# Joining the squares of k's four token blocks before the head norm matmul, in a kernel of two attention and two Fourier layers

## The chip, the core and the metric

The kernel runs on one core of a Trainium2 chip. The metric is the device time of one execution in microseconds (us); for the kernel before it is 2460.21 us, the median of three runs (2456.98 to 2460.39).

## What is computed

x has 2048 tokens of 640 features. Twice in a row it goes through an attention block and a Fourier block, each with a layer norm in front and a residual added.

```python
def _A_ref(x, wqkv, wo):                      # H = 32 heads of Dh = 20
    qkv = (x @ wqkv).reshape(B, S, 3, H, Dh) ...
    q, k, v = qkv[0], qkv[1], qkv[2]
    scores = einsum("bhqd,bhkd->bhqk", q, k) * (Dh ** -0.5)
    p = softmax(scores, axis=-1)
    o = einsum("bhqk,bhkd->bhqd", p, v)
    return o...reshape(B, S, D) @ wo
x = x + _A_ref(_layernorm(x), A_wqkv, A_wo)
x = x + _B_ref(_layernorm(x), ...)            # Real(DFT_seq(DFT_hidden(x)))
x = x + _A_ref(_layernorm(x), A_wqkv, A_wo)
x = x + _B_ref(_layernorm(x), ...)
```

The kernel doesn't look for the largest score of a row before it takes exponentials. It uses a bound instead: a score is no larger than the length of the head's q times the length of its k, so the largest squared norm of q and of k over all tokens, head by head, gives a shift that is safe for every row. These norms are what the change is about.

## The kernel before, in words

**Tiling.** Tokens are worked on in four blocks of 512 (NB = 4, the index tb), features in five chunks of 128 (ND = 5). q and k are held with features on partitions: a product of 15 matmuls (five feature chunks, three passes each, line 195) gives 128 features of q or of k for 512 tokens in one psum bank, the tile `pqk`. There are five such chunks of q (c = 0 to 4) and five of k (c = 5 to 9). A head has 20 features, so a chunk of 128 holds parts of seven or eight heads.

**keep** (line 198) takes a finished `pqk` out of psum as a rounded part and a remainder (the tile `hl`), has POOL issue the DMA that stores it in memory (line 211), and makes the squares `sq` in bf16. In the prologue ACT makes the rounded part and the squares (line 208) and VectorE the remainder (line 209); in the last token block ACT does the squares first. In the attention VectorE does all three in the order rounded part (line 88), remainder (line 91), squares (line 205).

**norms** (line 214) multiplies the squares by `ind`, a 0/1 matrix from 128 features to 32 heads (line 216): the result `pn`, 32 heads by 512 tokens in psum, holds each token's share of each head's squared norm. VectorE takes the maximum over the 512 tokens (line 217) into one column of `top`, which has a column for each of q and k, chunk and token block. **bounds** (line 434) takes the maximum over the blocks, adds over the chunks, and multiplies q's with k's. **bound** (line 442) makes the shift from it and sends it to memory for four heads; the loads of q take it from there as two further rows. At the end a flag is set if, for all 32 heads, the product stays within (30 / SCALE)^2 with SCALE = 20 ** -0.5 (line 426); the program runs its general path over both layers again if a flag is missing.

**Prologue** (line 279). Chunk 0 of q and chunk 0 of k are done for all four token blocks. In each block TensorE does two products, then turns the next block's x (line 167), then the two norms (line 363), then four value products `pv` of 15 matmuls; in the first block the value products come ahead of the turning. The last block has nothing to turn, so its norms follow the products directly. Psum tiles of the prologue go round eight banks, one further with each tile (line 161). After the last block come the first bound and its shift.

**Attention.** The steps go through 8 groups of four heads, 4 blocks of 512 queries and 16 tiles of 128 keys: 512 steps per layer. A step has two score tiles `psc` of two matmuls each (line 522), two exponentials on ACT (line 525) and four value matmuls into the accumulator `acc` (line 533), which stand side by side in four groups of 32 output columns. At the end of a query block VectorE transposes the accumulator (line 540) and scales it. psum holds three double banks for scores, one bank for `acc` and one, `fill`, for everything else.

The rest of q, k and v is made between these steps, on TensorE's instruction stream, in an order written out beforehand (lines 387 to 425): chunks 1 of k, 1 of q, 2 of k, 2 of q, then the second half of v, then 3 of k, 3 of q, 4 of k, 4 of q, each for four token blocks. Up to step 236 strings like "ssfsssvvsssvvsssfssvvsssnvv" say where scores (s), value matmuls (v), halves of a product (f) and the norm (n) stand; later a product comes in three pieces. The norm of a block is placed two steps behind its product up to step 236 and four steps behind it afterwards (line 641). VectorE also compares pieces of the transform matrices along the whole attention (lines 803 and 807). `fill` here is also the name of a pool of SBUF tiles, with one buffer for each tag, `hl` and `sq` among them.

Of the kernel before, what the change touches and what calls it, by code (L numbers as in the profile page):

```python
# [7 lines left out]
BF = mybir.dt.bfloat16  # L8
I32 = mybir.dt.int32
AF = mybir.ActivationFunctionType  # L10
OP = mybir.AluOpType
# [4 lines left out]
S, D, H, DH = 2048, 640, 32, 20  # L16
# [3 lines left out]
ND = D // 128  # L20
NT = S // 128
NB = S // 512
# [17 lines left out]
def mha_fnet_kernel(ctx, tc, x_in, wqk, wv, wo, seq, hid, nat_seq, nat_hid, out):  # L40
# [33 lines left out]
    def bank(tag, shape, name):  # L74
        return pools["pool"].tile(list(shape), F32, name=name, tag=tag)
# [60 lines left out]
    class Qkv:  # L136
        def __init__(s, L, src):
            s.L, s.src = L, src
            s.xn, s.xt, s.rs, s.v = {}, {}, {}, {}
            s.scr = {qk: dr.tile([D, 2, S], F32, name=f"scr{qk}_{L}") for qk in "qk"}  # L140
            s.shift = {n: dr.tile([H, 2, c], F32, name=f"shift{n}_{L}") for n, c in (("b", 512), ("m", S))}
            s.n = 1
            s.made, s.raw, s.silent = set(), {}, False
# [54 lines left out]
        def keep(s, p, c, tb, vector, room):  # L198

            hl = room("hl", [2, 512], F32R, "hl")  # L200
            sq = room("sq", [512], BF, "sq")
            h = hl[:, 0].bitcast(F32)
            if vector:
                split(hl[:, 0], hl[:, 1], p, vector)
                V.tensor_tensor(sq, h, h, op=OP.mult)
            else:
                for f, x in ((AF.Copy, hl[:, 0]), (AF.Square, sq))[::-1 if tb == NB - 1 else 1]:
                    A.activation(x, p, f)
                V.tensor_tensor(hl[:, 1], p, h, op=OP.subtract)
            k, c = divmod(c, ND)  # L210
            G.dma_start(s.scr["qk"[k]][c * 128:(c + 1) * 128, :, tb * 512:(tb + 1) * 512], hl.bitcast(F32))  # L211
            return sq

        def norms(s, p, c, tb, sq):

            PE.matmul(p, ind[:, c % ND], sq, start=True, stop=True)  # L216
            V.tensor_reduce(s.top[:H, c // ND, c % ND, tb:tb + 1], p, op=OP.max, axis=AX.X)  # L217

# [60 lines left out]
        def prologue(s, vals, xt, fill, att):  # L279
# [50 lines left out]
            for tb in range(NB):  # L330

                sq, late = [], tb == 0
                if late:
                    for k in range(2):
                        later(tb, k, s.load)
                for k in range(2):
                    p = s.bank([128, 512], "pqk")
                    for dc in range(ND):
                        for f in s.product(p, s.w[k], tb, dc):
                            f()  # L340
                    sq.append(s.keep(p, k * ND, tb, False, (room, fill)[k]))
                    if late:
                        s.stats(2 + k)
                        continue
                    later(tb, k, s.stats)
                if late:
                    for n in range(4):
                        own(tb, n)
                        if n < 2:
                            s.norm(2 + n)  # L350
                            later(tb, n, s.stats)
                if tb == 0:
                    att.setup()
                elif tb == 1:
                    for t in range(NT - ND, NT):
                        ones(t)
                if tb + 1 < NB:
                    s.turn(tb + 1)
                    for k in range(2):
                        later(tb + 1, k, s.load)  # L360
                for k in range(2):
                    later(tb, k, s.norm)
                    s.norms(s.bank([H, 512], "pn"), k * ND, tb, sq[k])
                if tb == 0:
                    att.qload(0, 0, None)
                elif tb == 1:
                    s.fetch(ND + 1)
                    for j in range(2):
                        att.kload(0, 0, j)
                elif tb == 2:  # L370
                    s.w1 = s.weights(s.fill("w", [2, ND, 128], F32R, "wqk"), ND + 1, True)
                    s.fetch(1)
                    att.zeros(room)
                elif tb == NB - 1:
                    list(s.bound(0, room))
                    att.qshift(0, 0)
                    for j in range(2):
                        att.kload(0, 1, j)
                if not late:
                    for n in range(4):  # L380
                        own(tb, n)
# [3 lines left out]
        def work(s):  # L385

            order = [ND + 1, 1, ND + 2, 2, ND + 3, 3, ND + 4, 4]
            w = {0: s.w1}

            def chunk(i):  # L390
                c = order[i]
                for tb in range(NB):
                    p = bank("fill", [128, 512], "pqk")
                    for more in pieces([s.product(p, w[i], tb, dc) for dc in range(ND)], 8 if (i, tb) < (5, 1) else 5):
                        if more:
                            yield True
                    sq = s.keep(p, c, tb, True, s.fill)

                    def after():
                        s.norms(bank("fill", [H, 512], "pn"), c, tb, sq)  # L400
                        s.made.add((c, tb))
                        if tb == NB - 1:
                            s.made.add(c)
                            if i + 1 < len(order):
                                w[i + 1] = s.weights(s.fill("w", [2, ND, 128], F32R, "wqk"), order[i + 1], True)
                            if i + 2 < len(order):
                                s.fetch(order[i + 2])
                    yield after

            for i in range(4):  # L410
                yield from chunk(i)
            for t in range(NT):
                p = bank("fill", [128, HD], "pv")
                for more in pieces([s.value(p, t, dc) for dc in range(ND)], 15):
                    if more:
                        yield True
                s.own(p, t, 1, True)
                yield None
            s.made.add("v")
            for i in range(4, 8):  # L420
                yield from chunk(i)

            s.silent = True
            r = s.bounds()
            ok = const.tile([128, 1], F32, name="ok", bufs=2)
            V.tensor_scalar(ok[:H], r[:H, 2:3], (GUARD / SCALE) ** 2, None, op0=OP.is_le)

            def after():
                p = bank("fill", [1, 1], "pok")
                PE.matmul(p, ok[:H], one[:H], start=True, stop=True)  # L430
                V.tensor_scalar(s.flag, p, float(H), None, op0=OP.is_equal)
            yield after
# [1184 lines left out]
```

## Time and profile before

| | |
|---|---|
| median of three runs | 2460.21 us (2456.98 to 2460.39) |
| the profiled execution | 2460.17 us, span of its instructions 2458.3 us |
| TensorE's granted clock | 0.998 of full speed |
| TensorE, ACT, VectorE, POOL busy | 99%, 86%, 40%, 21% of the span |
| norm matmuls and their maxima | 80 of each, 30.1 us and 53.6 us |

Engines are named as in the profile: PE is TensorE, PEld its weight loads, DVE is VectorE, ACT the scalar engine, POOL GpSimd, and SP the queue that issues most loads. A row of the timeline gives start, duration, engine, line, operation, output and inputs, and how many instructions are merged in it. A matmul's end in the profile is modelled and reaches into its successors, so what one costs is read from start to start. A row of groups gives the busy time, the mean of one in ns, and the idle time before it. A row of the windows gives the stretch, its length, the busy time and count of PE, PEld, DVE, ACT and POOL (or of those engines alone on which the tile asked for is used), the clock and the DMA's share.

### The profile page before, as it was taken

To read this page: it belongs to the slowest core of one execution; us is meant where nothing else is said; L and a number is where in the kernel's file an instruction comes from. 1 tells how busy PE (TensorE), PEld (TensorE's weight loads), DVE (VectorE), ACT (ScalarE), POOL (GpSimd) and SP (SyncE) were. 2 spreads that over 40 slices of the span, in tenths; PEclk is the share of its full clock that TensorE was granted. 3 is DMA by queue.
4 is the path that set the end of the run, shared out by engine and by line. 5 is a ranking of instruction groups with operands and counts; after the bars stand their busy time and mean duration, and the time that the engine had idled before them with its cause. 6 is when DMAs were issued, how large, how long until landed. Compare 5 with 4: busy or idle time off the path is not lost. (4 is left out here: it accounts for less than half of the span.)

```text
span 2458.3 us, 43836 instructions
## 1 busy us (share of the span) xinstructions
PE 2428.5 (99%) x16350; PEld 1174.1 (48%) x16350; DVE 995.3 (40%) x2198; ACT 2117.6 (86%) x2428; POOL 527.7 (21%) x1032
## 2 busy tenths in 40 slices
PE   8999999999999999999999999999999999999997
PEld 7644444443333333349885444454433333333596
DVE  6244442234343333427763444323333232323275
ACT  6699998899999999995457989888999999999762
POOL 2012211112111212115321212211112212222143
PEclk9999999999999999999999999999999999999999
DMA  5324231223232225318552332312222322252274
GB/s 184 101 89 126 81 113 51 77 69 109 74 96 89 88 86 168 96 44 284 193 182 96 112 102 85 117 53 69 79 82 57 93 64 68 57 151 83 67 255 185
DMA packets 128228, 262.64 MB, mean 107 GB/s; under 512 B 29937, under 2 KB 54289, under 8 KB 128005
## 3 DMA queue, kind: packets, MB, share of 16 engines
q1 hardware_dynamic: 89412, 159.89, 20.4%
q0 software_dynamic: 38592, 99.85, 12.8%
q8 instruction: 132, 2.16, 0.4%
q14 instruction: 92, 0.75, 0.1%
HBM read 175.29 MB, written 84.31 MB: 106 GB/s over the span
## 5 line engine op out<-in xcount | busy, mean ns | idle before, releaser
L525 ACT ACTIVATE e<-psc 128x1024 f32<-128x1024 f32 x2048 | 1919.4, 1059 | 109.9 <-PE psc L522 98.9
L533 PE MATMUL acc<-e,v 128*32 128x512 f32 x8192 | 1034.2, 600 | 0.4 <-DVE of L540 0.4
L522 PE MATMUL psc<-stq,stk 62*128 62x512 f32 x4096 | 745.3, 445 | 2.3 <-ACT e L525 1.1
L522 PEld LDWEIGHTS psc<-stq,stk 62*128 62x128 f32 x4096 | 333.9, 184 | 704.2 <-ACT e L525 563.8
L533 PEld LDWEIGHTS acc<-e,v 128*32 128x32 f32 x8192 | 217.5, 108 | 396.3 <-issue 357.5
L103 PE MATMUL pqk<-xt,wqk 128*128 128x512 f32 x1200 | 319.4, 407 | 0.5 <-ACT xt L90 0.2
L554 POOL DMA_DIRECT2D o<-oh x256 | 131.2, 521 | 828.7 <-DVE oh L549 816.8
L88 DVE CAST hl<-pqk 128x512 fp32r<-128x512 f32 x64 | 44.3, 692 | 597.8 <-PE pqk L103 597.8
L103 PEld LDWEIGHTS pqk<-xt,wqk 128*128 128x128 f32 x1200 | 213.1, 188 | 84.1 <-issue 39.6
L103 PE MATMUL pv<-wv,xt 128*128 128x320 f32 x960 | 151.3, 313 | 0.0
L103 PEld LDWEIGHTS pv<-wv,xt 128*128 128x128 f32 x960 | 141.1, 188 | 15.5 <-issue 9.7
L554 POOL DMA_DIRECT2D o<-ot x256 | 128.2, 509 | 1.8 <-issue 0.9
L540 DVE STREAM_TRANSPOSE of<-acc 128x512 f32<-128x512 f32 x64 | 45.8, 715 | 199.2 <-PE acc L533 199.2
L211 POOL DMA_DIRECT2D scrq<-hl x40 | 28.3, 706 | 429.6 <-DVE hl L91 240.1
L211 POOL DMA_DIRECT2D scrk<-hl x40 | 27.7, 693 | 390.1 <-DVE hl L91 280.6
L96 PE MATMUL py<-wo,o 128*128 128x320 f32 x320 | 101.3, 316 | 2.3 <-DVE xr L1007 1.3
L217 DVE TENSOR_REDUCE top<-pn 32x1 f32<-32x512 f32 x80 | 53.6, 677 | 121.0 <-PE pn L216 120.6
L803 DVE TENSOR_REDUCE far<-cq 128x1 f32<-128x512 f32 (+5 forms) x169 | 98.5, 584 | 5.7
L98 PE MATMUL py<-wo,o 128*128 128x320 f32 x320 | 99.1, 310 | 1.0 <-DMA o<-o 1.0
L97 PE MATMUL py<-wo,o 128*128 128x320 f32 x320 | 98.7, 308 | 0.0
L807 DVE TENSOR_TENSOR cq<-cq 128x512 f32<-128x512 f32 (+4 forms) x166 | 96.3, 580 | 4.2 <-DMA cq<-in_nat_seq_dram 3.5
L247 DVE COPY v<-pv 128x320 f32<-128x320 f32 x32 | 15.7, 489 | 161.3 <-PE pv L103 161.3
(201 smaller groups left out, 1750.7 us busy)
## 6 DMA issues: line engine op xcount, KB each, us to landing
cq<-in_nat_seq_dram POOLq DMA_DIRECT2D x64, 512.0 KB, 5.4
scrq<-hl POOLq DMA_DIRECT2D x40, 512.0 KB, 3.2
scrk<-hl POOLq DMA_DIRECT2D x40, 512.0 KB, 3.2
stq<-scrq SPq DMA_DIRECT2D x256, 80.0 KB
stk<-scrk SPq DMA_DIRECT2D x128, 160.0 KB
o<-o SPq DMA_DIRECT2D x32, 384.0 KB
stq<-scrq SPq DMA_DIRECT2D x256, 40.0 KB
stk<-scrk SPq DMA_DIRECT2D x128, 80.0 KB
```

What stands on the lines that cost most here:

```text
L96: PE.matmul(out_ap, ah, bh, start=start, stop=False)
L97: PE.matmul(out_ap, ah, bl, start=False, stop=False)
L98: PE.matmul(out_ap, al, bh, start=False, stop=stop)
L103: yield lambda i=i, j=j, k=k: PE.matmul(out_ap, a[i], b[j], start=dc == 0 and k == 0, stop=dc == ND - 1 and k == 2)
L211: G.dma_start(s.scr["qk"[k]][c * 128:(c + 1) * 128, :, tb * 512:(tb + 1) * 512], hl.bitcast(F32))
L217: V.tensor_reduce(s.top[:H, c // ND, c % ND, tb:tb + 1], p, op=OP.max, axis=AX.X)
L522: PE.matmul(p[:, i], s.k[g, kc // 8, j][r, kc % 8 * 128:(kc % 8 + 1) * 128], s.q[g, qb, j][r], start=True, stop=True)
L525: A.activation(e, p, AF.Exp, scale=SCALE)
L533: PE.matmul(s.acc[32 * j:32 * j + 32], s.a.v[kc][:, v0:v0 + 32], s.e[n, j // 2][:, j % 2], start=kc == 0, stop=kc == NT - 1, skip_group_ch ...
L554: G.dma_start(s.o[k, h * DH:(h + 1) * DH, qb * 512:(qb + 1) * 512], hl[k][32 * j:32 * j + DH])
L803: V.tensor_reduce(to, x, op=OP.max, axis=AX.X, apply_absolute_value=True)
L807: V.tensor_tensor(y, x, y, op=op)
```

## The change

k's squares are no longer summed for each token block by itself. For a k chunk, one `sq` tile lives through the four token blocks: the first block writes its squares into it, the following ones join theirs by an elementwise maximum, and only the last block runs the norm matmul and its maximum over the free axis. Column j of `sq` then holds, feature by feature, the largest square among tokens j, 512 + j, 1024 + j and 1536 + j. The sum of it over a head's features is at least each of these tokens' squared norms, so it is still a bound, and a wider one. q is as it was: four norms per chunk.

In the prologue ACT writes the later blocks' squares into the place of the remainder (`hl[:, 1]`), VectorE takes the maximum, and then the remainder is written there. In the attention the squares of a later k block are made on VectorE in two halves of 256 columns in a small tile of its own, `sqh`, each half followed by its maximum. `norms` now takes a psum tile only when it runs, so in the prologue the rotation of the banks is one shorter in the first three blocks.

```diff
         def keep(s, p, c, tb, vector, room):
             hl = room("hl", [2, 512], F32R, "hl")
-            sq = room("sq", [512], BF, "sq")
+            k, c = divmod(c, ND)
+            if not (k and tb):
+                s.sq[k] = room("sq", [512], BF, "sq")
+            sq = s.sq[k]
             h = hl[:, 0].bitcast(F32)
             if vector:
                 split(hl[:, 0], hl[:, 1], p, vector)
-                V.tensor_tensor(sq, h, h, op=OP.mult)
+                if not (k and tb):
+                    V.tensor_tensor(sq, h, h, op=OP.mult)
+                else:
+                    own = room("sqh", [256], BF, "sqh")
+                    for i in (slice(0, 256), slice(256, 512)):
+                        V.tensor_tensor(own, h[:, i], h[:, i], op=OP.mult)
+                        V.tensor_tensor(sq[:, i], sq[:, i], own, op=OP.max)
             else:
-                for f, x in ((AF.Copy, hl[:, 0]), (AF.Square, sq))[::-1 if tb == NB - 1 else 1]:
+                own = hl[:, 1, :256].bitcast(BF) if k and tb else sq
+                for f, x in ((AF.Copy, hl[:, 0]), (AF.Square, own))[::-1 if tb == NB - 1 else 1]:
                     A.activation(x, p, f)
+                if k and tb:
+                    V.tensor_tensor(sq, sq, own, op=OP.max)
                 V.tensor_tensor(hl[:, 1], p, h, op=OP.subtract)
-            k, c = divmod(c, ND)
...
         def norms(s, p, c, tb, sq):
+            if c >= ND and tb < NB - 1:
+                return
+            p = p([H, 512], "pn")
             PE.matmul(p, ind[:, c % ND], sq, start=True, stop=True)
...
-                    s.norms(s.bank([H, 512], "pn"), k * ND, tb, sq[k])
+                    s.norms(s.bank, k * ND, tb, sq[k])
...
-                        s.norms(bank("fill", [H, 512], "pn"), c, tb, sq)
+                        s.norms(lambda *a: bank("fill", *a), c, tb, sq)
```

More of the change, by code (lines that the diff above doesn't have):

```diff
@@ L138, in __init__ @@
             s.L, s.src = L, src
-            s.xn, s.xt, s.rs, s.v = {}, {}, {}, {}
+            s.xn, s.xt, s.rs, s.v, s.sq = {}, {}, {}, {}, {}
             s.scr = {qk: dr.tile([D, 2, S], F32, name=f"scr{qk}_{L}") for qk in "qk"}
```

## The prediction, made before the change was built

> **What bounds the kernel now.** I read the page's busy shares first, then the windows of the first layer by stage, then the list of waits, and last the timeline around single norm matmuls.
>
> ```profile
> span 2458.3 us, 43836 instructions
> PE 2428.5 (99%) x16350; PEld 1174.1 (48%) x16350; DVE 995.3 (40%) x2198; ACT 2117.6 (86%) x2428; POOL 527.7 (21%) x1032
> ...
> 87.20:350.00 262.80, 261.90 (x1759) 115.13 (x1761) 107.79 (x225) 238.95 (x254) 50.37 (x88) 1.00 0.33 102
> 560.00:930.00 370.00, 369.80 (x2529) 130.49 (x2527) 138.84 (x298) 364.02 (x390) 76.07 (x137) 1.00 0.29 89
> ...
> PE psc L522 <- ACT e L525: 1.1, 2, 0.5
> ACT e L525 <- PE psc L522: 98.9, 218, 0.9
> ```
>
> The span is 2458.3 us and the profiled execution took 2460.17, so 1.9 us lie around the span; the median of the three runs is 2460.21, the same to 0.04 us, and I reckon from 2460.17. TensorE is busy 99% of it. The two window rows are PE, PEld, DVE, ACT, POOL of two stretches of layer 1's attention. In the early one (87 to 350) ACT is busy 239 of 263 us, so TensorE sets the pace; in the later one (560 to 930) both are nearly full, 369.8 and 364.0 of 370. The waits agree: ACT waited 98.9 us for score products, while TensorE waited 1.1 us for ACT by name (a matmul that is held inside the pipe would not show, so this alone proves nothing). VectorE has 60% of the span free.
>
> So a matmul that goes is worth what it delays TensorE's stream, and VectorE's work is free unless TensorE waits for it.
>
> **What goes: 30 norm matmuls.** Each layer has 40 norm matmuls (80 in the program, in the row below), 20 for q and 20 for k. Of k's 20, the last block of each of five chunks keeps its own: 15 go per layer, 30 in all, 6 of them in the two prologues (chunk 0, blocks 0 to 2) and 24 in the attention (chunks 1 to 4). With each goes its maximum over the free axis on VectorE.
>
> ```profile
> L216 PE MATMUL pn<-sq,ind 128*32 128x512 bf16 x80 | 30.1, 388 | 0.9 <-ACT sq L208 0.9
> L217 DVE TENSOR_REDUCE top<-pn 32x1 f32<-32x512 f32 x80 | 53.6, 677 | 121.0 <-PE pn L216 120.6
> ...
> 99.89 1.92 PE L533 MATMUL acc<-e,v 128*32 128x512 f32 x16
> 100.67 0.68 DVE L205 TENSOR_TENSOR sq<-hl 128x512 bf16<-128x512 f32 x1
> 101.75 0.96 PE L522 MATMUL psc<-stq,stk 62*128 62x512 f32 x6
> 102.64 0.39 PE L216 MATMUL pn<-sq,ind 128*32 128x512 bf16 x1
> 102.65 2.10 PE L533 MATMUL acc<-e,v 128*32 128x512 f32 x16
> 104.68 0.73 PE L522 MATMUL psc<-stq,stk 62*128 62x512 f32 x4
> ...
> 642.81 1.06 PE L533 MATMUL acc<-e,v 128*32 128x512 f32 x8
> 643.80 0.73 PE L522 MATMUL psc<-stq,stk 62*128 62x512 f32 x4
> 648.64 0.39 PE L216 MATMUL pn<-sq,ind 128*32 128x512 bf16 x1
> 648.65 1.24 PE L533 MATMUL acc<-e,v 128*32 128x512 f32 x8
> 649.82 0.50 PE L522 MATMUL psc<-stq,stk 62*128 62x512 f32 x2
> ```
>
> A norm matmul lasts 0.388 us, but that is not its price: the value matmuls behind it start 0.01 us later (102.64, then 102.65). The price is read from start to start. Sixteen value matmuls without a norm in front take 99.89 to 101.75, 1.86 us; with one, 102.64 to 104.68, 2.04 us. Difference 0.18. Eight of them: 642.81 to 643.80 is 0.99 us, with the norm 648.64 to 649.82 is 1.18, difference 0.19. So **0.18 us each** in the attention; the bounds are 0 (wholly beside the values) and 0.39 (wholly by itself).
>
> By the Trainium skill, TensorE: Matmul & The Clock Gate, section Part 3: Packing small matmuls, matmuls with 32 output columns run side by side when they stand in different column groups. The norm's 32 rows and the values' first 32 share a group, so that rule leaves about one pass of 512 columns as the price, and the trace's 0.18 agrees.
>
> The stretch from 560 to 930 us holds 12 norms (the second row below counts the matmuls and the maxima of the norm tile in it): by the order of line 387 the last three chunks, q3, k4 and q4. So chunks 1 to 3 of k fall earlier, where ACT has time to spare, and the whole 0.18 counts: 3 chunks x 3 blocks x 2 layers x 0.18 = 3.24 us. Chunk 4 falls in the full stretch. There the exponential's own pace is
>
> ```profile
> 677.33 3.77 ACT L525 ACTIVATE e<-psc 128x1024 f32<-128x1024 f32 x4
> ...
> 560.00:930.00 370.00, 4.67 (x12) 8.15 (x12) 1.00 0.29 89
> L525 ACT ACTIVATE e<-psc x2048: 1014/1032/1595, 87.2 to 2317.9; 128x1024 f32<-128x1024 f32 x187
> ```
>
> four back to back in 3.77 us with 1.03 for one, so (3.77 - 1.03) / 3 = 0.91 each; 390 instructions on ACT in 370 us are at most 356 us at that pace. There are 14 us of room per 370, so TensorE still leads on the mean, but right behind a norm the exponentials run without a gap. Part of a norm's 0.18 is then given back to ACT. I take 0.14 (bounds 0 and 0.18): 6 x 0.14 = 0.84 us.
>
> **The prologues.** Here a pair of norms stands between two products.
>
> ```profile
> 41.52 0.60 PE L216 MATMUL pn<-sq,ind 128*32 128x512 bf16 x2
> 42.05 9.13 PE L103 MATMUL pv<-wv,xt 128*128 128x320 f32 x60
> ...
> 76.65 0.60 ACT L208 ACTIVATE sq<-pqk 128x512 bf16<-128x512 f32 x1 [2.31 <-PE pqk L103]
> 77.14 0.59 ACT L208 ACTIVATE hl<-pqk 128x512 fp32r<-128x512 f32 x1
> 77.30 0.38 PE L216 MATMUL pn<-sq,ind 128*32 128x512 bf16 x1 [0.43 <-ACT sq L208]
> 77.61 1.14 PE L103 MATMUL pv<-wv,xt 128*128 128x320 f32 x6
> 77.77 0.69 DVE L209 TENSOR_TENSOR hl<-pqk,hl 128x512 fp32r<-128x512 f32 x1 [2.71 <-ACT hl L208]
> ...
> 1249.65 0.53 PEld L103 LDWEIGHTS pqk<-xt,wqk 128*128 128x128 f32 x3 [0.34 <-DVE xt L91]
> ```
>
> Two norms delay the next product by 42.05 - 41.52 = 0.53 us, one by 77.61 - 77.30 = 0.31, so the second is worth 0.22. Of six such places one is lost: after layer 2's first block the product waits for VectorE's transposed rows anyway (0.34 at 1249.65). 5 x 0.22 = 1.10 us.
>
> The psum rotation of the prologue moves on by one bank less per block. Eight allocations now reach further back in time, so no bank is freed later than it is wanted; I count it at nothing, with the evictions on ACT and VectorE as the cover.
>
> **What comes, on the path.** In the last block of a prologue nothing covers k's squares: ACT ends them at 77.25, the norm starts at 77.30, and the value product stands behind it. Now VectorE's maximum comes between. VectorE is free then (its next work begins at 77.77). An elementwise operation whose operands are all bf16 is not in the trace. The nearest rows:
>
> ```profile
> L807 DVE TENSOR_TENSOR cq<-cq 128x256 f32<-128x256 f32 x32 | 13.2, 412 | 0.0
> L205 DVE TENSOR_TENSOR sq<-hl 128x512 bf16<-128x512 f32 x64 | 43.6, 681 | 0.0
> L543 DVE RECIPROCAL rc<-rc 128x16 f32<-128x16 f32 x64 | 16.2, 253 | 2.2
> ```
>
> By elements it is the 0.68 of 512 elements, by bytes the 0.41 of 256 f32 elements; the row that reads as many bytes is the nearer one, and I take 0.41, ends 0.25 (what 16 elements take) and 0.68. With 0.04 for the extra hand-over (77.73, where ACT's copy ends, to 77.77) TensorE waits 0.45 us more, in two layers 0.90; with 0.68 it would be 1.44.
>
> By the Trainium skill, VectorE: DVE Perf Modes, section The perf-mode tier table, an elementwise operation on two tensors runs at double rate when all are 16 bits wide; with the formula of its errata section that is an estimate of (512/2 + 151) / 0.96 = 424 ns, and the sum would be the same to 0.03 us. No run here shows it yet.
>
> Behind that maximum on VectorE stand k's subtraction and the two norm maxima, and behind these the bound, its shift and a DMA for the first scores. The subtraction could start at 77.77 and now starts at about 77.75, so this chain moves by a tenth, less than the value products in front of the scores do. In blocks 1 and 2 the maximum delays the subtraction and so POOL's write of k, and behind that SP's load of the first keys, by the same half microsecond; the scores that read them stand behind all value products of blocks 1 to 3 (9 us each by the row at 42.05), which hide it.
>
> **What comes, beside the path.** In the attention, each of k's blocks 1 to 3 has four operations of 256 columns instead of one of 512. The chain is serial: at most 4 x 0.41 plus a gap of 2.2 / 64 = 0.03 after each, 1.76 us against 0.68. The write of k to memory stands ahead of it on VectorE and doesn't move. Only the last block's norm waits for the chain: it starts at 100.67 as in the row above, ends at 102.43 at the latest, and the norm is due at 102.64. It holds, by 0.2 us; in chunk 4 the norm is placed four steps behind the squares instead of two (line 641). In the blocks without a norm the work that TensorE next wants of VectorE is the accumulator's transpose at the end of a token block (line 540), and the maximum over the norm (0.677) that used to stand ahead of it is gone: +1.08 and -0.68 cancel nearly. Cost 0, covered by VectorE's free 60%; without that cover, 24 x 0.4 = 10 us of VectorE would be in TensorE's way.
>
> **Sum.** -3.24 - 0.84 - 1.10 + 0.90 = **-4.3 us: 2455.9 us**, 0.17% less.
>
> **The rivals.**
>
> *The norms lay wholly beside the values* (0 instead of 0.18), or ACT takes over the pace: only the prologues are left, -1.10 + 0.90 = -0.2, **2460.0 us**. For it: the norm's end lies inside the value matmuls. Against: the two start-to-start differences.
>
> *VectorE comes late.* Maximum at 0.68 in the prologue, and the chain of four at 0.6 each, ending 0.4 after the norm is due in 6 last blocks: +0.5 + 2.4, **2458.8 us**. Against it: the 0.41 row.
>
> *A norm costs its whole duration.* 24 x 0.39 and the prologue as above: -9.4 + (-0.2) = -9.6, **2450.6 us**. Against it: the norm and the values overlap by 0.38 us in the rows.
>
> *Slower: the joined bound trips the guard.* A sum of maxima is no less than the maximum of the sums, so k's bound grows. If, for one head, the bound of q times that of k passes (30 / SCALE)^2 = 18000, the flag goes out and the program computes both layers again by the general path. Worked out from the reference's inputs, the largest product is 11283 before and 15521 after, 14% short of the point. The price if it trips: 2048 exponentials at 0.91 again, at least 1860 us, so over **4300 us**. For it: with other random draws of the same kind the product passed 18000 in some; against it: these inputs.
>
> **How the numbers follow.** Forecast 0.62, from 2454.3 to 2457.5 with the unknown prices above; norms beside or ACT's pace 0.13; VectorE late 0.10; whole duration 0.08; guard or another wait 0.07. Forecast, the first and the second rival hold 0.85: from 2454.3 to 2460.0. The runs of before spread 3.4 us, mostly downwards, so I open the lower end to 2453.0 and the upper to 2460.2. A measurement of this kernel tells about 0.2%, 4.9 us, from no change; the forecast stands 0.6 us short of that. Some two in five of its chance (0.24, the lower end of its range) and the whole-duration case fall beyond: faster 0.32, same 0.61, slower 0.07.
>
> **What would show it.** 50 norm matmuls and as many maxima instead of 80; 2.75 us instead of 2.93 between score products where a k norm stood; a last norm of the prologue that waits for VectorE and not for ACT, some 0.45 us later; a 128x512 bf16 maximum near 0.42; k's last norm in a chunk still right behind its scores. It is wrong if ACT shows no gaps where it had them, if a norm names VectorE in the attention, or if anything runs after layer 2's last store.

## The result, and the profile after

The changed kernel takes 2455.39 us (median of 18 runs, 2452.39 to 2459.55), the kernel before 2458.73 us on the same chip (18 runs, 2456.98 to 2460.39): ratio 0.9985, 95% interval 0.9979 to 0.9991, so 0.15% less, with an interval that excludes no change. 2455.9 us were forecast, from 2460.17 for the kernel before. The two times lie 0.5 us apart, but the drop is 3.3 us where 4.3 were forecast: these 18 runs put the kernel before 1.4 us below the value that the forecast started from. The profiled execution of the changed kernel took 2458.13 us, 2.7 us above the median, with a span of 2456.3; it is one of the longer ones, and why is part of what follows.

First the page of the changed kernel, its span and busy times; then two stretches of its attention from the windows view (PE, PEld, DVE, ACT, POOL busy and count).

```profile
span 2456.3 us, 43826 instructions
PE 2425.9 (99%) x16320; PEld 1169.0 (48%) x16320; DVE 995.6 (41%) x2246; ACT 2116.0 (86%) x2428; POOL 529.0 (22%) x1032
```

```profile
87.20:350.00 262.80, 262.19 (x1765) 113.34 (x1764) 109.41 (x239) 239.62 (x255) 50.80 (x89) 1.00 0.32 102
560.00:930.00 370.00, 369.80 (x2529) 129.88 (x2527) 138.65 (x305) 364.82 (x391) 77.98 (x141) 1.00 0.28 88
```

Thirty matmuls are gone (16350 to 16320). In the early stretch TensorE gets through six instructions more in the same 262.80 us than before (x1759), although norms are missing from the count; in the late one it does as many as before (x2529). ACT has one instruction more in each. So the stream gets ahead in the early stretch; what it gains in the late one is too little to read from counts.

The answer for the tile `sq` of the changed kernel, then that for `pn` (duration in ns as min/median/max, first and last start), and that for `sqh`:

```profile
L230 PE MATMUL pn<-sq,ind x50: 376/389/390, 31.8 to 2139.2; 128*32 128x512 bf16 x50
L214 DVE TENSOR_TENSOR sq<-sq,sqh x48: 291/292/294, 117.4 to 2013.8; 128x256 bf16<-128x256 bf16 x48
...
L220 DVE TENSOR_TENSOR sq<-sq,hl x6: 424/426/426, 40.5 to 1295.6; 128x512 bf16<-128x512 bf16 x6
```

```profile
L231 DVE TENSOR_REDUCE top<-pn x50: 668/679/680, 33.8 to 2139.6; 32x1 f32<-32x512 f32 x50
its engine sat idle before it (us, times) until:
  PE pn L230: 76.4, 36
  DVE sq L220: 1.8, 2
```

```profile
L213 DVE TENSOR_TENSOR sqh<-hl x48: 412/420/426, 117.0 to 2013.3; 128x256 bf16<-128x256 f32 x48
```

50 norms and 50 maxima over them, as the change says; TensorE waits for a joined square in two places, the last norm of each prologue (L220, 2 times), and never for the squares of the attention (no row names L214). These two places are the added wait, here in the timeline of layer 1's last prologue block:

```profile
75.83 0.39 PE L230 MATMUL pn<-sq,ind 128*32 128x512 bf16 x1
75.98 1.09 ACT L218 ACTIVATE hl<-pqk 128x512 bf16<-128x512 f32 x2 [2.30 <-issue]
76.61 0.43 DVE L220 TENSOR_TENSOR sq<-sq,hl 128x512 bf16<-128x512 bf16 x1 [2.21 <-ACT hl L218]
77.09 0.38 PE L230 MATMUL pn<-sq,ind 128*32 128x512 bf16 x1 [0.88 <-DVE sq L220]
...
77.40 2.02 PE L103 MATMUL pv<-wv,xt 128*128 128x320 f32 x12
```

The second norm waits 0.88 us, for VectorE, where it waited 0.43 for ACT: 0.45 more, as forecast.

And a place of the early attention where a norm stood. Sixteen value matmuls start at 102.46 and the scores behind them at 104.31:

```profile
102.46 1.92 PE L547 MATMUL acc<-e,v 128*32 128x512 f32 x16
104.31 0.73 PE L536 MATMUL psc<-stq,stk 62*128 62x512 f32 x4
```

1.85 us, against 2.04 with the norm: 0.19.

**Where the time went, stage by stage.** The span is cut at the start of the first matmul of each kind; the numbers are us, two executions of each kernel ("again" is e2 for before and e1 for after). "Prologue" runs to the first score (in layer 2 from the first transpose), "chunks 1-3" to step 240, "chunk 4" from step 240 to step 448, "projection" from the last value matmul to the Fourier block's first product.

```
                 before  again    after  again    after - before
prologue 1        86.60  87.12    86.39  86.39    -0.21  -0.73
chunks 1-3       500.69 500.67   499.02 498.96    -1.67  -1.71
chunk 4          393.37 393.51   393.32 393.50    -0.05  -0.01
rest             121.69 121.70   121.69 121.72     0.00  +0.02
projection 1      60.96  60.92    62.21  58.84    +1.25  -2.08
Fourier 1         65.13  65.13    67.65  67.93    +2.52  +2.80
prologue 2        75.31  75.11    75.07  75.09    -0.24  -0.02
chunks 1-3       500.68 500.68   498.97 498.97    -1.71  -1.71
chunk 4          393.37 393.55   393.37 393.55     0.00   0.00
rest             121.69 121.71   121.67 121.71    -0.02   0.00
projection 2      59.71  59.18    60.30  60.45    +0.59  +1.27
Fourier 2         79.09  79.07    76.67  76.50    -2.42  -2.57
span            2458.29 2458.35 2456.34 2453.62   -1.95  -4.73
```

Three things are to be seen. Chunks 1 to 3 give 1.7 us in each layer, in both pairs; that is the change's main gain. Chunk 4 gives nothing. And two stages in which the change edits nothing moved by 2.5 us each, with opposite signs: the Fourier block of layer 1 is longer, that of layer 2 shorter. The projections scatter by up to 3.4 us from one execution to the next (62.21 and 58.84 for the same kernel), so a single span says little to 3 us. The first prologue scatters by 0.5 (86.60 and 87.12), which is of the size of what the change does there.

### The profile page after: what moved, and what is told of

It is laid out like the page before. It is cut to its first block, busy times and chain, and to the rows that moved or that the text cites. A ratio compares the mean times of both kernels' runs of the same rounds, so it can differ in the third digit from the quotient of the medians.

```text
span 2456.3 us, 43826 instructions
## 1 busy us (share of the span) xinstructions
PE 2425.9 (99%) x16320; PEld 1169.0 (48%) x16320; DVE 995.6 (41%) x2246; ACT 2116.0 (86%) x2428; POOL 529.0 (22%) x1032
## 3 DMA queue, kind: packets, MB, share of 16 engines
q8 instruction: 131, 2.15, 0.4%
## 5 line engine op out<-in xcount | busy, mean ns | idle before, releaser
L547 PEld LDWEIGHTS acc<-e,v 128*32 128x32 f32 x8192 | 211.0, 108 | 406.5 <-issue 368.6
L96 PEld LDWEIGHTS py<-wo,o 128*128 128x128 f32 x320 | 60.0, 188 | 10.2 <-issue 5.8
```

Of the source, the lines that this page charges most:

```text
L96: PE.matmul(out_ap, ah, bh, start=start, stop=False)
L547: PE.matmul(s.acc[32 * j:32 * j + 32], s.a.v[kc][:, v0:v0 + 32], s.e[n, j // 2][:, j % 2], start=kc == 0, stop=kc == NT - 1, skip_group_ch ...
```

## The experiments

My theory after the result: (a) a norm among value matmuls costs 0.19 us where TensorE leads and nothing to speak of where ACT is right behind; (b) the prologue gains its norms and pays 0.45 for the maximum; (c) the Fourier blocks moved because transfers from memory end at other times in each execution; when e1 and e2 had shown that they repeat, this gave way to another: they moved because the number of instructions changed, not the work. Rivals: the gain sits in other stages and only happens to have this size; the late chunk was won and lost again to VectorE's longer chain; the Fourier stages moved with VectorE's or POOL's order.

### e1 and e2: both kernels again

No edit.

> The changed kernel once more. Theory (TensorE's stream): the stages are the same to 0.1 us as in its first profile: first prologue 86.4, first attention up to step 240 499.0, steps 240 to 448 393.3, rest 121.7 us; the projections and Fourier stages (62.2 and 67.7 us in layer 1, 60.3 and 76.7 in layer 2) move by up to 3 us either way, because transfers from memory end there at other times in each execution. Rival (the change does something to these stages, by the moved SBUF tiles): they come out at 62.2, 67.7, 60.3 and 76.7 again. Time 0.9985 of before, 2455 us.

> The kernel before once more, to see what its stages do by themselves. Theory: prologue 86.6, attention 500.7, 393.4 and 121.7 us to 0.1 us; the projections and Fourier stages differ by up to 3 us from 61.0, 65.1, 59.7 and 79.1. Rival: these four are the same to 0.3 us, and then what the changed kernel showed there belongs to the change.

e1 took 2456.6 us, ratio 0.9989, interval 0.9980 to 0.9998; e2, one run, 2460.14. Their stages are the "again" columns above. The stages of attention repeat to 0.2 us, the Fourier blocks to 0.3, and keep their difference; the projections don't repeat. For the Fourier blocks the theory was wrong (a scatter of up to 3 us was expected), and in this the rivals were right: their shift belongs to the change. The 0.5 us between the two first prologues of the kernel before are there after 17 us, ahead of any norm.

### e3: the change in the attention alone

```diff
-            if not (k and tb):
+            if not (k and c and tb):
...
-            if c >= ND and tb < NB - 1:
+            if c > ND and tb < NB - 1:
```
and no maximum in the prologue.

> The joining only in the attention (k's chunks 1 to 4); chunk 0 in the prologue has its four norms as before. Theory: the prologue is back at 86.6 (it was 86.4 with the change), with the last norm waiting for ACT and not for VectorE; the attention keeps all of its gain: 499.0, 393.3, 121.7 in both layers. Total gain 3.4 us of the 3.8 that the stages of the change add up to. Rival (the prologue is where the gain is lost or made): the attention moves by more than 0.1 us.

2456.23 us in one run. Chunks 1 to 3 take 499.06 and 499.00, as with the whole change, and the prologues 86.53 and 75.05, within 0.15 of it. So the attention's gain doesn't need the prologue's edit, and the prologue's edit is nearly a draw. The last norm of the prologue waits for ACT again:

```profile
76.42 0.39 PE L228 MATMUL pn<-sq,ind 128*32 128x512 bf16 x1
77.23 0.38 PE L228 MATMUL pn<-sq,ind 128*32 128x512 bf16 x1 [0.43 <-ACT sq L218]
```

### e5 and e6: a norm twice, and half a norm

Both start from the kernel before. e5 runs each norm matmul that the change would take from chunks 1 to 4 a second time; e6 runs it over the first 256 tokens only, and so leaves out half of these tokens from the bound.

```diff
+            for _ in range(2 if c > ND and tb < NB - 1 else 1):
                 PE.matmul(p, ind[:, c % ND], sq, start=True, stop=True)
```
```diff
+            n = 256 if c > ND and tb < NB - 1 else 512
+            PE.matmul(p[:, :n], ind[:, c % ND], sq[:, :n], start=True, stop=True)
```

> The kernel before, with the norm matmul of k's blocks 0 to 2 run twice in the attention (24 more matmuls into the same result, no more maxima). Theory (a norm costs about one pass of 512 columns in its column group, 0.19 us, wherever TensorE leads): steps up to 240 take 500.7 + 9 x 0.19 to 0.22 = 502.5 us, and in chunk 4, where taking the norm away gained nothing, adding one still costs 0.19 to 0.22 each: 393.4 + 0.6 = 394.0. Rival 1 (in the late stretch ACT sets the pace and a norm there is free both ways): 393.4. Rival 2 (a norm lies wholly beside the values): 500.7 and 393.4.

> The kernel before, with the norm of k's blocks 0 to 2 in the attention over 256 of the 512 tokens only; it leaves out half of these tokens from the bound. Theory (in chunk 4 the whole gain is lost because the score pair that follows two pairs later then has to wait for its double bank, by 0.06, and loses the hidden load of its weights, 0.10): half a norm less moves that pair by 0.09 only, and it had 0.18 - 0.05 to spare, so there is no wait and chunk 4 gains more than with no norm at all: 393.37 - 3 x 0.09 = 393.1, against 393.3 with the norm gone. Up to step 240: 500.7 - 9 x 0.09 = 499.9. Rival (ACT sets the pace there): 393.35, and nothing to gain by any cut.

e5 took 2461.75 us, e6 2458.05. Chunks 1 to 3 of e5: 502.79 and 502.89, that is 2.1 and 2.2 us more than before for nine norms, 0.23 to 0.25 each, a little over the 0.19 to 0.22 expected. In the trace of e5 the second norm starts 0.21 us behind the values of the first:

```profile
102.54 0.39 PE L217 MATMUL pn<-sq,ind 128*32 128x512 bf16 x1
102.55 0.63 PE L534 MATMUL acc<-e,v 128*32 128x512 f32 x3
102.76 0.38 PE L217 MATMUL pn<-sq,ind 128*32 128x512 bf16 x1
102.98 1.88 PE L534 MATMUL acc<-e,v 128*32 128x512 f32 x13
```

e6: 499.77 and 499.72, 0.92 and 0.96 less, 0.10 to 0.11 each. So a norm's price there goes with its columns, and it's neither 0 nor 0.39: the third rival of the prediction is out, and the first is out for chunks 1 to 3.

In chunk 4, doubling costs 0.60 us in each layer (393.97) for three norms, 0.20 each (0.42 to 0.46 against the second execution of before), while taking the norm away wins 0.0. Half a norm (393.24 and 393.33) wins 0.13 and 0.04, inside the 0.2 that the stage scatters; so e6's expectation that half a norm gains more there than none stays undecided. Why adding costs there and removing doesn't give is read from the traces. A place of chunk 4 before, and the same place of the changed kernel, 1.9 us earlier:

```profile
708.75 0.73 PE L522 MATMUL psc<-stq,stk 62*128 62x512 f32 x4
709.41 0.39 PE L216 MATMUL pn<-sq,ind 128*32 128x512 bf16 x1
...
711.25 1.07 PE L533 MATMUL acc<-e,v 128*32 128x512 f32 x8
712.25 0.73 PE L522 MATMUL psc<-stq,stk 62*128 62x512 f32 x4
712.91 0.50 PE L103 MATMUL pqk<-xt,wqk 128*128 128x512 f32 x1
```

```profile
707.53 1.06 PE L547 MATMUL acc<-e,v 128*32 128x512 f32 x8
...
709.19 1.06 PE L547 MATMUL acc<-e,v 128*32 128x512 f32 x8
710.18 0.89 PE L536 MATMUL psc<-stq,stk 62*128 62x512 f32 x4
711.00 1.42 PE L103 MATMUL pqk<-xt,wqk 128*128 128x512 f32 x5
```

From the place of the norm to the product behind the second pair of scores: 709.41 to 712.91 is 3.50, 707.53 to 711.00 is 3.47. The norm's 0.19 is gone, but the four score matmuls at 710.18 take 0.82 instead of 0.66 until the next start. Their weight loads say why, first before, then in the changed kernel:

```profile
712.25 0.40 PEld L522 LDWEIGHTS psc<-stq,stk 62*128 62x128 f32 x4 [0.84 <-ACT e L525]
```

```profile
710.18 0.19 PEld L536 LDWEIGHTS psc<-stq,stk 62*128 62x128 f32 x2 [0.84 <-ACT e L539]
710.57 0.19 PEld L536 LDWEIGHTS psc<-stq,stk 62*128 62x128 f32 x2 [0.20 <-ACT e L539]
```

Before, the four loads follow one another; in the changed kernel the second pair's load stands 0.20 us more, until an exponential is done that still reads the double bank which these scores want. Once TensorE comes early there, it is given back: 0.16 of 0.19 in this place. The other five places go the same way: followed from start to start, TensorE is 0.17 to 0.19 us earlier right behind each missing norm of chunk 4, and 0.05 or less some 4 us later, in both pairs of executions.

### e7: late squares

From the changed kernel: the multiplication on VectorE runs three times instead of once in the last block of a k chunk, so the joined squares come later.

```diff
+                        for _ in range(3 if tb == NB - 1 else 1):
                             V.tensor_tensor(own, h[:, i], h[:, i], op=OP.mult)
```

> The change, with each square of k's last block in the attention made three times over (four more operations of 256 columns on VectorE, some 0.45 us each), so that the chain ends 1.8 us later. In the change it ends 0.44 us ahead of the norm up to step 240 and 3.5 us ahead in chunk 4. Theory (VectorE costs nothing until the norm waits for it, and then TensorE waits in full): the norm names VectorE in 6 places, 1.4 us each; up to step 240 499.0 + 3 x 1.4 = 503.2 us per layer, 393.3 in the late stretch unchanged. Rival (the wait is hidden by what TensorE has in its queue): 499.0.

2466.86 us in one run; chunks 1 to 3 take 503.33 and 503.43, 4.3 and 4.5 us more than in the changed kernel, 1.44 and 1.49 for each of three chunks; chunk 4 doesn't move (393.50, 393.69). The list of waits names VectorE at six norms:

```profile
PE pn L231 <- DVE sq L215: 8.3, 6, 1.4
```

So the chain on VectorE does end close ahead of the norm in chunks 1 to 3, and has room in chunk 4; the rival that chunk 4 lost its gain to the longer chain is out, since there a still longer one costs nothing. How much room the change left is in its own timeline of VectorE, and in TensorE's row for the norm:

```profile
552.35 0.41 DVE L213 TENSOR_TENSOR sqh<-hl 128x256 bf16<-128x256 f32 x1
552.80 0.29 DVE L214 TENSOR_TENSOR sq<-sq,sqh 128x256 bf16<-128x256 bf16 x1
553.13 0.43 DVE L213 TENSOR_TENSOR sqh<-hl 128x256 bf16<-128x256 f32 x1
553.59 0.29 DVE L214 TENSOR_TENSOR sq<-sq,sqh 128x256 bf16<-128x256 bf16 x1
```

```profile
554.32 0.39 PE L230 MATMUL pn<-sq,ind 128*32 128x512 bf16 x1
```

The chain takes 1.53 us and ends at 553.88, 0.44 ahead of the norm. With this and the 426 ns of the maximum in the prologue the prediction's second rival, VectorE late, is out too.

### e8: the old rotation of the banks

From the changed kernel: where a k norm is left out in the prologue, the rotation moves on by a bank all the same, as before the change.

```diff
             if c >= ND and tb < NB - 1:
+                s.n += c == ND
                 return
```

> The change, with the prologue's psum rotation moved on by one bank where a norm was dropped, so that every product has the bank that it had before the change. Theory: one value product per prologue waits again for the transposed rows of the bank (0.08 us more: prologue 86.5 instead of 86.4), and the second pair of the first scores no longer waits for the last value product's copy (0.35 us earlier, without any effect on what follows). Rival (the rotation is worth nothing): 86.4.

2458.34 us in one run; the prologues take 87.22 and 75.79, 0.83 and 0.72 more than in the changed kernel, where 0.1 was expected. I had costed the rotation at next to nothing. With the old one, the second value product of the second block takes the bank of the transposed rows, while VectorE, which has the maximum to do first, begins to split them at 43.97 instead of 43.59:

```profile
41.76 2.46 PE L103 MATMUL pv<-wv,xt 128*128 128x320 f32 x15
44.71 2.02 PE L103 MATMUL pv<-wv,xt 128*128 128x320 f32 x12 [0.49 <-DVE xt L91]
```

In the changed kernel these products run on from 41.68 without a gap. So "psum taken only when the norm runs" isn't tidying: without it, the prologue's edit would lose some 0.5 us in each layer (0.6 and 0.1 against the two executions of before in layer 1, 0.5 and 0.7 in layer 2).

### e4: k ahead of q in the last prologue block

From the changed kernel: in the last block k's product comes first, so that q's product covers the maximum; the norms follow in the same order.

```diff
+                ks = (1, 0) if tb == NB - 1 else (0, 1)
...
-                for k in range(2):
+                for k in ks:
```

> The change, but in the last block of each prologue k's product, squares and norm stand ahead of q's, so that VectorE's maximum runs while TensorE works on q's product. Theory: the wait for the maximum (0.45 us per layer) is gone and only the 0.43 for q's squares on ACT stays, as before the change: prologue 85.9 and 0.45 less in layer 2 as well, 0.9 us less than the change, 2454.3 us if the change is at 2455.2. Rival (the first scores wait for the bound's chain or for q's last write to memory, which now come later): the prologue stays at 86.4.

The prologues did what was asked: 86.04 and 74.80, 0.35 and 0.27 less. But the time was 2457.99 us, ratio 0.9993, interval 0.9984 to 1.0002, no better than the changed kernel's 2456.6 in the same runs: layer 2's attention lost 1.4 us in chunks 1 to 3 (500.38) and 1.7 in chunk 4 (395.05), layer 1's nothing. 2454.3 us were expected, and the loss by no theory. Among its exponentials there is a pause of 0.28 us on ACT once in every 64 of them (numbers 1074, 1138, 1202 and so on in the changed kernel, two exponentials later in e4). ACT has four instructions fewer before layer 2's attention in e4 (2397 for 2401 in the trace), and the pause had moved from an exponential that TensorE doesn't wait for to one whose bank it wants next. In e4 the exponential behind the six scores at 1423.64 starts at 1424.52, 0.88 us behind them, and TensorE then stops at 1427.43:

```profile
1423.64 0.97 PE L537 MATMUL psc<-stq,stk 62*128 62x512 f32 x6
1424.52 4.69 ACT L540 ACTIVATE e<-psc 128x1024 f32<-128x1024 f32 x5 [1.05 <-PE psc L537]
...
1426.39 0.74 PE L537 MATMUL psc<-stq,stk 62*128 62x512 f32 x4
1427.43 0.50 PE L537 MATMUL psc<-stq,stk 62*128 62x512 f32 x2 [0.30 <-ACT e L540]
```

### e9: TensorE's instruction fetch moved back

The trace records, among the DMA packets, blocks of 16 KB of kind "instruction" (q8): 131 in the changed kernel, with 32640 matmuls and weight loads on TensorE, and 132 before, with 32700, so one for about 250 of them. Here is the time of the nearest one, counted from the issue of three loads at the Fourier block's seam (`craw`, of the sequence transform):

```
             fetch, layer 1   Fourier 1    fetch, layer 2   Fourier 2
before          -1.57 us        65.13         +1.87 us        79.09
before again    -1.59           65.13         +2.81           79.07
e6              -1.79           65.14         +2.18           80.13
e5              -4.55           65.19         -4.69           76.47
after           +2.85           67.65        +10.84           76.67
after again     +1.83           67.93        +15.24           76.50
e3              +2.95           67.78         +9.88           76.53
e4              +1.69           67.78        +15.26           76.58
e8              +2.27           68.68        +15.09           76.48
e7              +1.72           69.10        +15.27           76.35
e10             +2.81           66.40        +14.94           76.80
```

A fetch 1.7 to 3.0 us behind the issue goes with a Fourier block that is 1.3 to 4.0 us longer, every other place on record (4.7 to 1.6 us ahead of it, or 4.2 and more behind, e9 and e11 included) with the short one. The place says whether, not by how much: +2.85 goes with 67.65 us, +2.81 in e10 with 66.40. With fewer instructions of TensorE ahead of the seam the fetch comes later, with more of them (e5) earlier. The change, with 30 instructions of TensorE fewer per layer (15 norms and a weight load each), moved the fetch into this stretch in layer 1 and out of it in layer 2. To test it: 15 matmuls of one column with their weight loads, whose result isn't read, ahead of layer 1's projection.

```diff
+            if s.next.tag == "0":
+                p = bank("b0", [H, 512], "pad")
+                for _ in range(15):
+                    PE.matmul(p[:, :1], ind[:, 0], ind[:, 0, 0:1], start=True, stop=True)
```

> The changed kernel, with 15 matmuls of one column and a weight load each (30 instructions of TensorE, as many as the change takes out of a layer) at the start of layer 1's projection; their result isn't read. Theory (the 2.6 us that layer 1's Fourier part lost and layer 2's won come from where TensorE's fetch of its next 16 KB of instructions falls against the three loads at the seam): the fetch of layer 1 lies ahead of these loads again, so layer 1's Fourier part takes 65.1 us instead of 67.7, layer 2's stays at 76.5, and the pads cost at most 0.9 us in a projection of 58.8 to 62.2; in sum 1.7 to 2.6 us less than the changed kernel, about 2453. Rival (the longer Fourier part comes from something else that the change moved, VectorE's or POOL's order): layer 1's Fourier part stays at 67.7 and the time rises by the pads.

2454.6 us (11 runs), ratio 0.998, interval 0.9971 to 0.9989. The fetch stands at -1.96 in layer 1 and +4.46 in layer 2; Fourier 1 takes 65.16 us, Fourier 2 76.49. The rival is out: VectorE's and POOL's work is that of the changed kernel, and Fourier 1 is short all the same. By the medians e9 is 5.2 us under the kernel before, 1.6 us more than 2453 expected. ACT's rows at this seam, in the changed kernel and then in e9, show the late load:

```profile
1174.93 2.18 ACT L1217 ACTIVATE chl<-craw 128x512 fp32r<-128x512 f32 x4
1181.68 1.16 ACT L1217 ACTIVATE chl<-craw 128x512 fp32r<-128x512 f32 x2 [4.56 <-DMA craw<-in_seq_dram]
```

```profile
1173.81 2.18 ACT L1221 ACTIVATE chl<-craw 128x512 fp32r<-128x512 f32 x4
1178.90 1.15 ACT L1221 ACTIVATE chl<-craw 128x512 fp32r<-128x512 f32 x2 [2.91 <-DMA craw<-in_seq_dram]
```

ACT works on the four pieces that are there already from 1174.93 and 1173.81; the next come 6.75 and 5.09 us after these times, so 1.66 us later in the changed kernel. And the DMA's own rows, from the issue of the three loads (1176.52) for 5.2 us in the changed kernel, and from their issue (1175.39) for 3.5 us in e9:

```profile
q1 hardware_dynamic: 366, 1.37, 79.5%
q8 instruction: 1, 0.02, 1.2%
```

```profile
q1 hardware_dynamic: 219, 0.83, 66.0%
```

The block of instructions is among the packets of the one and not of the other. The loads' queue as a whole was not slower: it moved 1.37 MB in 5.2 us and 0.83 MB in 3.5. By the Trainium skill, Runtime: NRT & Kernel Launch, section Instruction fetch mechanics, the sequencer fetches 16 KiB blocks of 256 instructions by a DMA queue of its own, and the cost is mostly hidden. The trace agrees with the blocks (2.15 MB in 131) and with their being hidden for TensorE, which is busy 99% of the span; but the loads beside this one came later. By what path one block of 16 KB holds up three loads of 512 KB isn't shown here.

### e10 and e11: ACT's instruction count, and both together

e10 is e4 with two ACT instructions of one column more in each prologue, whose result isn't read; e11 is e10 with the matmuls of e9.

```diff
                 elif tb == NB - 1:
+                    for _ in range(2):
+                        A.activation(s.top[64:96, 0, 0, 0:1], one[64:96], AF.Copy)
                     list(s.bound(0, room))
```

> The kernel with k ahead of q in the last prologue block, and two ACT instructions more of one column in each prologue, whose result isn't read, which give ACT back the four instructions that this order had saved by layer 2's attention. Theory (layer 2's attention lost 1.4 and 1.7 us there because ACT's pause of 0.28 us, once in 64 exponentials, had moved onto exponentials that TensorE waits for): layer 2's stretches are 499.0 and 393.4 us again instead of 500.4 and 395.05, while the prologues keep their gain (86.0 and 74.8). Rival (the order of the norms itself, with q's maximum last, disturbs layer 2): they stay at 500.4 and 395.

> Both together: k ahead of q in the last prologue block, ACT's two instructions per prologue, and the 15 one-column matmuls ahead of layer 1's projection. Theory: prologues 0.6 us less in sum than in the changed kernel, layer 1's Fourier part 65.1 us, layer 2's attention 499.0 and 393.4; about 2452.5 us, 0.9972 of the kernel before, with the projections' scatter of 2 us. Rivals: Fourier part 67.7 (2455) or layer 2's attention 3.1 us longer (2455.5).

e10 took 2453.25 us in one run: prologues 85.66 and 74.58, layer 2's chunks 499.03 and 393.31. The loss of e4 is gone with four instructions that compute nothing, and the pause is back on numbers 1074, 1138 and so on. The prologues are 0.38 and 0.22 shorter than in e4, which wasn't expected; almost all of it arises in the first 25 us of each prologue, ahead of the edit. The same place as in e4's rows above, in e10, where the exponential starts 0.60 us behind the scores:

```profile
1420.14 0.97 PE L539 MATMUL psc<-stq,stk 62*128 62x512 f32 x6
1420.74 5.61 ACT L542 ACTIVATE e<-psc 128x1024 f32<-128x1024 f32 x6 [0.48 <-PE psc L539]
...
1422.89 1.26 PE L539 MATMUL psc<-stq,stk 62*128 62x512 f32 x6
```

No stop in the six scores. The rival (the order of the norms) is out; that the pause goes by ACT's instruction count is shown, that it is ACT's instruction fetch is only argued, from its period (64 exponentials and as many semaphore instructions).

e11: 2452.32 us (6 runs, 2450.66 to 2452.92), ratio 0.997 to the kernel before, interval 0.9958 to 0.9982. Its stages in the profiled execution (span 2448.9): prologues 85.59 and 74.57, Fourier 65.15 and 76.56, layer 2's chunks 499.03 and 393.37. It beats both kernels by the medians, before by 7.5 us in the same runs; against the changed kernel, which stood in other runs, the stages say 0.8 + 0.5 + 2.5 = 3.8 us, beside projections that happened to be 3.7 us shorter.

The prediction's last rival, a joined bound that trips the guard, did not come up with these inputs: nothing runs after layer 2's last store. No run makes it trip.

## Why the prediction was right, and where it wasn't

The mechanism of the main term was right, one term was mis-sized, and the time came out in part by luck. Here is the steps' own sum on the trace, against -4.3 us. To see the steps, take the start of each matmul that both kernels have, and follow how the difference between the kernels grows.

- **18 norms in chunks 1 to 3**: 0.18 each forecast, 3.24; measured 1.67 + 1.71 = 3.38, 0.19 each. Right, and e5 and e6 say that it is the norm matmul itself.
- **6 norms in chunk 4**: 0.14 each, 0.84 forecast; measured 0.05 and, again, 0.01. This is the mis-sized term, and the lower bound (0) was the value; there the first rival's figure came true. I reasoned from the mean (14 us of room per 370) that TensorE leads. Locally it doesn't: two score pairs behind the norm, a double bank isn't free yet, and a held pair pays twice, for the wait and for a weight load that is no longer hidden. The wait shows in PEld's row at 710.57; among TensorE's matmuls the list of waits has 0.5 us for ACT's exponentials in the whole run. That the late load hides no longer is read from the starts (0.10 of the 0.16), not tested by itself.
- **Norms of the prologue**: 5 x 0.22 = 1.10 forecast. All six gave, 0.21 to 0.25 each, 1.35 in sum; the one counted as lost, behind layer 2's first block, gave 0.21 as well: the wait of 0.34 at 1249.65, for which it was counted out, is in one execution of the kernel before and not in the other. The rotation, counted at nothing, gave 0.08 more in each layer, where a value product had waited for the transposed rows' bank; e8 shows that with the maximum in place it's worth 0.7 to 0.8. That I left it at nothing was wrong, though no forecast time hung on it.
- **The maximum ahead of the last norm**: 2 x 0.45 forecast; measured 0.45 and 0.44, with an instruction of 426 ns where I took 0.41. By the Trainium skill, VectorE: DVE Perf Modes, section The perf-mode tier table, the estimate was 424 ns; the trace agrees.
- **VectorE's chain beside the path**: forecast 1.76 us, 0.2 ahead of the norm; measured 1.53 and 0.44. No norm names VectorE in the attention. Right, and e7 shows what hung on it: every microsecond that the chain is later than this room is paid three times a layer.
- **Sum of these steps** (chunks 1 to 3, chunk 4, the prologues' norms, the rotation, the maximum): -3.4 - 0.05 - 1.35 - 0.16 + 0.89 = -4.1 us; the table's stages in which the change edits something give -3.9 and -4.2. That it is so near to the -4.3 forecast is two misses that offset, 0.8 too much in chunk 4 and 0.4 too little in the prologues. It stands against -3.3 between the medians and -3.7 (interval -5.2 to -2.2) by the ratio.

What the prediction didn't see is outside its steps: 2.5 us lost in layer 1's Fourier block and 2.5 won in layer 2's, by 30 instructions fewer in each layer, which move the fetches (e9 tests this in layer 1; in layer 2 it rests on the table). They cancel, so the forecast time came out; by luck, since nothing in the sum spoke of it, and by luck too in that the forecast started 1.4 us too high. With the fetch in another place the same change would have measured some 2.5 us better (e9, by its Fourier stage) or, as far as the table of fetches tells, as much worse.

## What to carry to other kernels

Price a small matmul from start to start, not by its duration, and price it anew in each stage: where the engine behind it is within a few hundredths of the pace, what is removed comes back as a wait, and what is added still costs. When an edit of a few tenths moves a stage that it doesn't touch, compare stages of two executions each and look at what depends on the mere number of instructions before blaming the edit. A wait on the path can often be covered by reordering (k ahead of q, 0.3 us a layer), but the reordering has to be timed as a whole.

## What the runs showed of the hardware that was not expected

- One fetch of 16 KB of TensorE's instructions, 1.7 to 3.0 us behind the issue of three loads of 512 KB, goes with a stage that is 1.3 to 4.0 us longer (65.13 to 66.40 in e10, where the fetch stands at +2.81, to 69.10 in e7), in all 13 profiles and both layers; 30 idle instructions moved it away (e9).
- ACT pauses 0.28 us once in 64 exponentials; whether it costs nothing or 0.28 each time depends on which exponential it meets, and four instructions more or fewer decide it: 3.1 us in a layer (e4 against e10).
- A norm of 0.39 us between value matmuls costs 0.19, half of its columns half of that (0.10 to 0.11 less, by e6), and a second one right behind 0.23 to 0.25.
- An all-bf16 maximum takes 292 ns for 256 elements and 426 for 512; the multiplication from f32 to bf16 of 256 elements takes 420.
